# Chunks of 64 tokens instead of 128 in a delta-rule kernel: attention products as 64x64 tiles, and an inverse grown from diag(beta)

## Chip, cores and metric

The kernel runs on one core of a Trainium2 chip. The metric is the device time of one execution in microseconds (us). PE is TensorE, DVE is VectorE, ACT is ScalarE, POOL is GpSimd.

## The reference

Four batch elements with eight heads, 768 tokens and head size 48 go through the delta rule in float32. The result, 3072 tokens of width 384, goes through a block gated by a cosine with a hidden width of 2048.

```python
k_n = k / (np.linalg.norm(k, axis=-1, keepdims=True) + 1e-06)
for t in range(S):                       # state: (B, H, D, D)
    y[:, :, t] = q_t @ state
    v_old = k_t @ state
    state = state + beta_t * outer(k_t, v_t - v_old)
x = y.transpose(0, 2, 1, 3).reshape(B * S, H * D)
h = x @ w_in
out = (h * cos(h)) @ w_out               # float32
```

## The kernel before

In a chunk of C = 128 tokens, u = (I + A)^-1 (beta v - beta K S), y = Q S + mask(Q K^T) u and S += K^T u, where A is the part of beta K K^T below the diagonal. The inverse X is built from diagonal blocks that double in size. A *unit* is one chunk of one batch element with its 8 heads; there are 24. Two heads of size 48, padded to 64, share the 128 partitions. The even and odd heads ("parities") form two chains:

```python
def gram(par, lhs, rhs, name):                 # 64 rows, 128 columns
    rows = slice(DP * par, DP * par + DP)
    p = bank("att", [128, NP, 128], name)
    for j in range(NP):                        # NP = 4 heads of this parity
        nc.tensor.matmul(p[:, j], lhs[rows, j], rhs[rows, j])
    return p
# ... a = gram(kb_t, k_t), xt and x: identity minus pairs, by masks on DVE and POOL
for i, m in enumerate(LEVELS):                 # 2, 4, 8, 16, 32, 64
    for j in range(NP):
        nc.tensor.matmul(p_w[:, j], a[:, j], xt[:, j])
    nc.vector.tensor_tensor(out=wt, in0=p_w, in1=mask4(4 + i), op=ALU.mult)
    yield
    for j in range(NP):
        nc.tensor.matmul(p_xt[:, j], x[:, j], wt[:, j])
    # ... p_x = wt^T x, except at the last level
    nc.vector.tensor_tensor(out=xt, in0=xt, in1=p_xt, op=ALU.subtract)
    nc.vector.tensor_tensor(out=x, in0=x, in1=p_x, op=ALU.subtract)
    yield
```

Three streams are merged by their `yield`s: this preparation of unit n+1, the recurrence over chunks of unit n, and the gated block of two finished units (`p_h = w_in^T x`, the cosine on ACT and DVE, `p_o = g^T w_out`). The compiler's scheduler then orders each engine's instructions again: ready work of a later step may fill a gap.

## Time and profile before

| | before |
|---|---|
| time, median of 3 runs | 1667.6 us (1667.6 to 1669.3) |
| period of a unit in the steady part | 64.9 us |
| units 0 to 3 (the opening) | 287.6 us |
| PE busy in the span | 95% |

The period is the distance between the first query transposes of units 4 and 23 in the timeline, over 19. These are windows of the trace of the kernel before, one in the opening and one in the steady part; the columns are the window, its length, each engine's busy time with its number of instructions, the granted clock, DMA's share and its rate:

```profile
core 0: us, PE busy (x) PEld busy (x) DVE busy (x) ACT busy (x) POOL busy (x), PEclk, DMA share, GB/s
...
100.00:200.00 100.00, 84.92 (x564) 80.16 (x565) 91.95 (x184) 5.63 (x11) 31.86 (x27) 0.80 0.21 60
...
400.00:600.00 200.00, 199.31 (x1436) 176.84 (x1435) 104.13 (x167) 36.65 (x63) 35.45 (x30) 1.00 0.06 13
```

In the opening DVE is the busiest engine, 92 of 100 us, since it also narrows the weights.

### The profile page before, as it was taken

How to read it: one execution, taken by the hardware profiler on the slowest of the kernel's cores; microseconds unless marked ns; L12 is line 12 of the kernel's file. 1: busy time of each engine (PE TensorE's matmuls, PEld its weight loads, DVE VectorE, ACT ScalarE, POOL GpSimd, SP SyncE). 2: the span in 40 equal slices, each digit the busy share in tenths (PEclk: the TensorE clock that was granted, in tenths of full speed). 3: DMA queues.
4: the chain of work that ended last, by engine and by line, in shares of the span. 5: the costliest groups of instructions: out<-in, count | busy, mean ns of one | idle time of the engine just before them, and what ended most of it. 6: DMA issues, size and time to landing. Idle time of an engine off the chain costs nothing.

```text
span 1665.8 us, 25603 instructions
## 1 busy us (share of the span) xinstructions
PE 1588.9 (95%) x11214; PEld 1418.7 (85%) x11214; DVE 936.8 (56%) x1559; ACT 309.9 (19%) x530; POOL 326.8 (20%) x291
## 2 busy tenths in 40 slices
PE   4778989999999999999999999999999999999998
PEld 3778889889889889889889889989988988988965
DVE  4999866456456446446546545545545645644612
ACT  1010022122112112112203202202202202211222
POOL 7242250220220211202202202102122022011000
PEclk9978879999999999999999999999999999999999
DMA  7222000000000000000000000000000000000000
GB/s 161 85 72 76 25 15 6 15 15 6 20 15 6 20 15 6 20 15 6 10 19 12 10 10 20 10 10 20 10 11 20 1 10 6 1 6 6 1 10 10
DMA packets 82673, 33.87 MB, mean 20 GB/s; under 512 B 75744, under 2 KB 78816, under 8 KB 82560
## 3 DMA queue, kind: packets, MB, share of 16 engines
q1 hardware_dynamic: 82560, 32.22, 8.0%
q8 instruction: 88, 1.44, 0.4%
q14 instruction: 25, 0.20, 0.0%
HBM read 27.49 MB, written 4.72 MB: 19 GB/s over the span
## 4 chain that ended last, share of the span: by engine, by line
PE 78%; DVE 10%; POOL 6%; ACT 2%; issue 2%; DMA 0%; POOLq 0%; SPq 0%
PE p_o L422 15%; PE p_xt L288 14%; PE p_w L282 13%; PE p_h L393 13%; PE p_x L292 11%; PE p_y L363 2%; POOL xt L270 2%; POOL x L273 2%; PE p_u L329 1%; PE p_a L260 1%; POOL x L272 1%; PE p_t L247 1%; PE p_y L354 1%; PE p_qk L260 1%; DVE wt L284 1%
## 5 line engine op out<-in xcount | busy, mean ns | idle before, releaser
L288 PE MATMUL p_xt<-wt,x 128*128 128x128 f32 x2304 | 313.6, 281 | 24.1 <-DVE wt L284 23.7
L282 PE MATMUL p_w<-xt,a 128*128 128x128 f32 x2304 | 302.9, 281 | 24.6 <-POOL xt L270 19.9
L282 PEld LDWEIGHTS p_w<-xt,a 128*128 128x128 f32 x2304 | 285.5, 196 | 45.2 <-POOL xt L270 23.2
L288 PEld LDWEIGHTS p_xt<-wt,x 128*128 128x128 f32 x2304 | 289.4, 194 | 38.6 <-DVE wt L284 32.6
L284 DVE TENSOR_TENSOR wt<-p_w,masks 128x512 f32<-128x512 f32 x288 | 194.1, 688 | 208.1 <-PE p_w L282 207.9
L393 PE MATMUL p_h<-x_ffn,w_in 128*128 128x256 f32 x1152 | 280.5, 386 | 6.6 <-DVE g L414 6.1
L422 PE MATMUL p_o<-w_out,g 128*128 128x384 f32 x768 | 264.9, 488 | 0.9 <-DVE g L414 0.9
L292 PE MATMUL p_x<-x,wt 128*128 128x128 f32 x1920 | 255.5, 276 | 0.0
L393 PEld LDWEIGHTS p_h<-x_ffn,w_in 128*128 128x128 f32 x1152 | 211.1, 194 | 33.9 <-issue 4.6
L292 PEld LDWEIGHTS p_x<-x,wt 128*128 128x128 f32 x1920 | 235.7, 193 | 0.0
L293 DVE TENSOR_TENSOR xt<-xt,p_xt 128x512 f32<-128x512 f32 x240 | 164.4, 685 | 76.4 <-PE p_xt L288 75.8
L422 PEld LDWEIGHTS p_o<-w_out,g 128*128 128x128 f32 x768 | 138.5, 190 | 78.8 <-PE p_h L393 1.3
L404 DVE SCALAR_TENSOR_TENSOR r<-turns,p_h 128x512 f32<-128x512 int32 x96 | 66.0, 687 | 218.6 <-ACT turns L402 218.6
L297 DVE TENSOR_TENSOR x<-x,p_x 128x512 f32<-128x512 f32 x240 | 163.9, 683 | 24.4 <-PE p_x L292 21.9
L237 POOL TENSOR_TENSOR kb<-kp,bt 128x384 f32<-128x384 f32 x24 | 24.6, 1028 | 646.1 <-PE p_t L247 646.0
L402 ACT ACTIVATE turns<-p_h 128x512 int32<-128x512 f32 x96 | 57.3, 597 | 376.3 <-PE p_h L393 343.5
L230 POOL TENSOR_TENSOR knrm<-ksum,half 128x8 f32<-128x8 f32 x24 | 39.8, 1661 | 277.8 <-DVE ksum L226 277.8
L414 DVE TENSOR_TENSOR g<-r,p_h 128x512 f32<-128x512 f32 x96 | 65.7, 684 | 44.3 <-ACT r L411 42.8
L272 POOL TENSOR_TENSOR x<-a,masks 128x512 f32<-128x512 f32 x48 | 61.5, 1281 | 146.0 <-ACT a L266 143.6
L410 ACT ACTIVATE r<-r 128x512 f32<-128x512 f32 x96 | 60.5, 631 | 109.2 <-DVE r L407 109.2
L407 DVE SCALAR_TENSOR_TENSOR r<-turns,r 128x512 f32<-128x512 int32 x96 | 69.6, 725 | 0.5
L411 ACT ACTIVATE r<-r,halfpi 128x512 f32<-128x512 f32 x96 | 69.3, 722 | 2.8
(76 smaller groups left out, 1335.8 us busy)
## 6 DMA issues: line engine op xcount, KB each, us to landing
pairs<-in_moe_w_in_dram SPq DMA_DIRECT2D x12, 512.0 KB, 4.0
pairs<-in_moe_w_out_dram SPq DMA_DIRECT2D x16, 384.0 KB, 3.1
kp<-in_k_dram SPq DMA_DIRECT2D x24, 192.0 KB, 2.8
qp<-in_q_dram SPq DMA_DIRECT2D x24, 192.0 KB, 2.8
vp<-in_v_dram SPq DMA_DIRECT2D x24, 192.0 KB, 2.6
out_dram<-o SPq DMA_DIRECT2D x24, 192.0 KB, 1.9
masks<-mask_consts SPq DMA_DIRECT2D x1, 640.0 KB, 3.9
beta_rows<-in_beta_dram SPq DMA_DIRECT2D x1, 96.0 KB, 4.2
```

Source lines behind the costliest of these rows:

```text
L272: nc.gpsimd.tensor_tensor(out=x, in0=a, in1=mask4(2), op=ALU.mult)
L282: nc.tensor.matmul(p_w[:, j], a[:, j], xt[:, j])
L284: nc.vector.tensor_tensor(out=wt, in0=p_w, in1=mask4(4 + i), op=ALU.mult)
L288: nc.tensor.matmul(p_xt[:, j], x[:, j], wt[:, j])
L292: nc.tensor.matmul(p_x[:, j], wt[:, j], x[:, j])
L293: nc.vector.tensor_tensor(out=x_t[:, par] if last else xt, in0=xt, in1=p_xt, op=ALU.subtract)
L297: nc.vector.tensor_tensor(out=x, in0=x, in1=p_x, op=ALU.subtract)
L393: nc.tensor.matmul(p_h[:, i], w_in[:, t, (f + i) * 128 : (f + i + 1) * 128], x[:, t], start=(t == 0), stop=(t == KT - 1),)
L404: nc.vector.scalar_tensor_tensor(out=r, in0=turns, scalar=-PI2_HI, in1=p_h, op0=ALU.mult, op1=ALU.add)
L407: nc.vector.scalar_tensor_tensor(out=r, in0=turns, scalar=-PI2_LO, in1=r, op0=ALU.mult, op1=ALU.add)
L411: nc.scalar.activation(r, r, AF.Sin, bias=halfpi, scale=-1.0)
L422: nc.tensor.matmul(p_o, gs[f // 4][:, f % 4, i * C : (i + 1) * C], w_out[:, f], start=(f == 0), stop=(f == FT - 1),)
```

## The change

A chunk is 64 tokens, and two batch elements fill the 128 partitions, one in each half. Every attention product is then a 64x64 tile, placed by the row half of its operands and the partition half of its output. The inverse starts at X = diag(beta) on the plain Gram matrix, so beta k, its transposes and the POOL masks go. The core of the diff:

```diff
-C = 128
-LEVELS = (2, 4, 8, 16, 32, 64)
+C = 64
+LEVELS = (1, 2, 4, 8, 16, 32)
...
+    TILES = ((0, 0), (1, 1), (0, 1), (1, 0))      # (row half, output half)
...
+        for j in range(NP):
+            for par, i in TILES:
+                nc.tensor.matmul(p_g[half(i), par, j],
+                    kq_t[rows48(par), 0, j, half(i)], kq_t[rows48(par), :, j, half(i)])
...
+        def product(p, lhs, rhs):
+            for h in range(H):
+                for i in range(2):
+                    nc.tensor.matmul(
+                        p[half(i), h], flat(lhs)[half(i), h], flat(rhs)[half(i), h])
+        xt = x = dg                                # diag(beta)
+        for n_level, m in enumerate(LEVELS):
+            p_w = bank("one", [128, H, C], "p_w")
+            product(p_w, g, xt)
+            nc.vector.tensor_tensor(out=flat(wt), in0=p_w, in1=mask8(2 + n_level), op=ALU.mult)
+            yield
+            product(p_x[:, 0], x, wt)
+            if not last:
+                product(p_x[:, 1], wt, x)
+            # ... xt_new = xt - p_x[:, 0]; x_new = x - p_x[:, 1]
```

The recurrence is rewritten in the same way: `p_kq` for K S and Q S and `p_s` for the state's update use all four TILES, `p_u` and the rest of y the two diagonal ones. The gated block is unchanged.

## The prediction

> **What bounds the kernel now.** I first read the page's busy shares and the slices, then its chain that ended last, then the groups by line, and last the timeline of a steady stretch. The busy shares and the chain:
>
> ```profile
> span 1665.8 us, 25603 instructions
> PE 1588.9 (95%) x11214; PEld 1418.7 (85%) x11214; DVE 936.8 (56%) x1559; ACT 309.9 (19%) x530; POOL 326.8 (20%) x291
> PE 78%; DVE 10%; POOL 6%; ACT 2%; issue 2%; DMA 0%; POOLq 0%; SPq 0%
> ```
>
> PE is busy 95% of the span with 11,214 matmuls and as many weight loads, and 78% of the last chain is PE. DVE is at 56%, DMA nowhere. So the kernel is bound by PE, and the question is only what one matmul instruction costs. The groups by line:
>
> ```profile
> L288 PE MATMUL p_xt<-wt,x 128*128 128x128 f32 x2304 | 313.6, 281 | 24.1 <-DVE wt L284 23.7
> L282 PE MATMUL p_w<-xt,a 128*128 128x128 f32 x2304 | 302.9, 281 | 24.6 <-POOL xt L270 19.9
> L393 PE MATMUL p_h<-x_ffn,w_in 128*128 128x256 f32 x1152 | 280.5, 386 | 6.6 <-DVE g L414 6.1
> L422 PE MATMUL p_o<-w_out,g 128*128 128x384 f32 x768 | 264.9, 488 | 0.9 <-DVE g L414 0.9
> L292 PE MATMUL p_x<-x,wt 128*128 128x128 f32 x1920 | 255.5, 276 | 0.0
> ```
>
> The program has 24 units x 2 parities x 6 levels x 4 heads = 1152 products p_w, the profile 2304: an fp32 product is two PE instructions, each with its own weight load. I call such a load with its matmul a pair. The means (281, 386, 488 ns) are latencies that overlap; the cost is the distance between starts, which the timeline gives:
>
> ```profile
> 704.08 1.03 PE L337 MATMUL p_s<-u,kp 128*128 128x96 f32 x8
> 704.95 1.08 PE L288 MATMUL p_xt<-wt,x 128*128 128x128 f32 x8
> 705.87 1.06 PE L292 MATMUL p_x<-x,wt 128*128 128x128 f32 x8
> 706.76 1.06 PE L288 MATMUL p_xt<-wt,x 128*128 128x128 f32 x8
> 707.65 1.06 PE L292 MATMUL p_x<-x,wt 128*128 128x128 f32 x8
> 709.44 2.75 PE L422 MATMUL p_o<-w_out,g 128*128 128x384 f32 x8
> ```
>
> Eight p_xt start at 706.76 and the next group at 707.65: 0.89/8 = 0.111 us a pair. p_s, with only 96 moving columns, takes the same (0.87/8), so up to 128 columns a pair costs the load of its 128 stationary columns. p_o: (2.75-0.488)/7 = 0.323 us for 384 columns. p_h: the same timeline has 12 in 2.76 us, (2.76-0.386)/11 = 0.216. A unit of 128 tokens and 8 heads thus has 48 Gram pairs, 272 of the inverse and 56 of the recurrence, 376 x 0.111 = 41.7 us; 15 transposes (one instruction each) x 0.109 = 1.6; the gated block 48 x 0.216 + 32 x 0.323 = 20.7. The sum is 64.0 us; units in the steady part follow each other every 64.8 us (first transpose of a unit at 288 us, nineteen units later at 1520). So PE time explains the period with 0.8 us left over. 21 such periods are 1361 us; the other 305 us are the opening, where DVE narrows the weights (in the table of windows DVE is busy 92 of the 100 us from 100 us on), and the tail.
>
> **What the Trainium skill says.** "TensorE: Matmul & The Clock Gate", section LDWEIGHTS: a weight load takes its column count over 1.2 ns, whatever the rows; 128 columns give 106.7, and the 109 to 111 ns above agree. So 64 columns should give some 53. The same page, Part 3, The mechanism: matmuls in different row groups run at the same time, starting some 4 ns apart. The kernel before shows it where its two parities (row halves) meet in the Gram products:
>
> ```profile
> 684.33 0.72 PE L260 MATMUL p_at<-kb_t,k_t 64*128 64x128 f32 x5
> 685.00 0.27 PE L260 MATMUL p_a<-k_t,kb_t 64*128 64x128 f32 x1
> 685.00 0.27 PE L260 MATMUL p_at<-kb_t,k_t 64*128 64x128 f32 x1
> 685.11 0.27 PE L260 MATMUL p_a<-k_t,kb_t 64*128 64x128 f32 x1
> 685.11 0.27 PE L260 MATMUL p_at<-kb_t,k_t 64*128 64x128 f32 x1
> ```
>
> Alone, five p_at in a row are 0.11 us apart; here a p_a of the other half starts with each, so two pairs go in 0.11 us. "TensorEngine Tiling (Array Packing)", Key Properties: changing the tiling mode drains the engine. The trace agrees: from the last p_o at 686.76 + 1.56 - 0.49 = 687.83 to the first 64-row p_qk at 688.25 it takes 0.42 us instead of 0.32, and the next p_qk another 0.1 late; leaving again costs as much, some 0.35 us for a round trip (estimate). Lastly the first page's section "Wait — 56ns, not 53.3ns?" gives a floor of about 25 ns from start to start of matmuls, and about 62 ns each if the sequencer decodes in software. No stretch of this trace keeps a rate above two pairs in 0.11 us, so it doesn't show the floor.
>
> **The change part by part.** A unit is still 1024 token-heads (64 tokens, 16 heads of two batch elements), so there are still 24 units, and the gated block keeps its 80 pairs and 20.7 us.
>
> - Inverse: 16 products of 64x64 for 8 of 128x128. Pairs: (16x6 + 16x6 + 16x5) x 2 = 544 instead of 272. The two batch elements sit in the two row halves and alternate, so two run at once. At half the columns a pair takes 0.056 us in its half, and 0.028 with two halves. I take 0.033, for imperfect pairing: 544 x 0.033 = 18.0 us instead of 30.2.
> - Gram: one set of 16 products (32 pairs) with 128 moving columns, instead of 24 (48 pairs): 32 x 0.111/2 = 1.8 us instead of 5.3.
> - Recurrence: 64 + 32 + 32 + 32 = 160 pairs instead of 56: 5.3 us instead of 6.2.
> - Transposes: 11 instead of 15, 1.2 us.
> - Mode changes: small products now stand between pieces of the gated block at some 9 places a unit instead of 2: 9 x 0.35 = 3.2 us, instead of 0.7.
> - PE in sum: 18.0 + 1.8 + 5.3 + 1.2 + 20.7 + 3.2 = 50.2 us.
> - DVE (off the path): 17 steps of the inverse instead of 34 at 0.69 us, so 11.7 instead of 23.5; the gated block's r, r, g 4 x 2.1 = 8.4; the rest some 3: 23 us of a 50 us unit.
> - POOL loses three mask operations of 1.3 us of each parity and is far off the path. DMA moves the same bytes in packets of the same 192 bytes; each transfer is split in two.
> - New waits: there is one chain a unit instead of two that take turns. A level is p_w 1.1, mask 0.7 + 0.4 of latency, half of p_x 1.1, subtraction 0.7 + 0.4: 4.4 us; six levels 26, with the norms, transposes and Gram ahead some 35 us. That is shorter than 50, and the schedule fills gaps with the gated block (the p_o group of 8 is split into 4 and 4 around the Gram products at 683 to 688 us). The single buffer shared by p_w, p_u and p_z, and DVE's queue, leave some gaps open: I put 3 us a unit, chosen, not measured.
>
> A period is then 53 us. Outside the 21 periods, the opening three units lose 3 x 17 x 0.69 = 35 us of DVE work and some PE work: 305 - 45 = 260. The time is 21 x 53 + 260 = **1373 us**.
>
> **Rivals.**
>
> 1. The two halves do not overlap in a sustained way. A pair is 0.056 us, attention 736 x 0.056 = 41 us as before, and a unit 1.2 + 20.7 + 41 + 4 = 67: 1670 to 1720 us, nothing won. For it: only short stretches of overlap are seen. Against it: there it is complete.
> 2. The issue of instructions becomes the bound: 827 matmuls a unit instead of 471, with loads. At 0.045 us a pair the period is some 61 us, the time some 1550. For it: no rate like it is in the trace, and the floors cited.
> 3. The single chain's waits become the bound: PE has 29 us of attention and 21 of filler, but fillers come at the wrong moments. If half of 12 waits of 1.1 us stay open, a unit is 57 us and the time 1455.
> 4. Everything works at 0.028 with few gaps: 48 us a unit, 1265 us.
>
> **Range and chances.** The four give 1265 to 1720; I hold the overlap likely (it was seen) at a rate between 0.028 and 0.045. Hence 1370, 8 in 10 from 1265 to 1560. Faster by over 2% (below 1634) fails only in rival 1 or with rivals 2 and 3 together: 0.88; within 2% 0.05; slower 0.07.
>
> **What would show each step.** Starts of p_w and p_x in the timeline, two at once, 32 in 1.0 to 1.1 us, confirm the rate; 1.8 us for 32 shows rival 1, an even 40 to 50 ns between single starts rival 2. The period between first transposes should be 50 to 57 us. PE idle before p_x on DVE wt should be 1 to 4 us a unit; much more is rival 3. DVE's busy time should fall from 937 to some 640 us, the inverse's DVE steps from 816 to 408 in number. PE instructions should be some 19,900. The prediction is wrong if a 64-column load costs more than half a 128-column one, or if mode changes cost much more than 0.35 us.

## More of the kernel before

In the steady part PE is never free: 199.3 of 200 us.

## The result, and the profile after

The changed kernel takes 1239.2 us (median of 4 runs, 1237.4 to 1245.5). Its ratio to the kernel before is 0.743, 95% interval 0.742 to 0.745. A ratio here is the mean time of one kernel's fast runs over that of the other's of the same rounds, so it is not quite the ratio of the medians. The change is faster by a quarter, and the time lies below the lower end of the predicted range (1265).

| | before | predicted | after |
|---|---|---|---|
| period of a unit, us | 64.9 | 53 | 46.9 |
| the rest, span less 21 periods, us | 303 | 260 | 250 |
| opening (units 0 to 3), us | 287.6 | | 229.4 |
| DVE busy, us | 937 | 640 | 611 |

So nearly the whole miss is in the period: 21 x 6.1 = 128 us. From the page after, the busy shares, the chain that ended last and the largest groups:

```profile
span 1235.5 us, 41854 instructions
...
PE 1136.5 (92%) x19669; PEld 888.0 (72%) x19669; DVE 611.4 (49%) x1113; ACT 283.6 (23%) x482; POOL 132.8 (11%) x137
...
PE 80%; ACT 2%; DVE 1%; issue 0%
...
L433 PE MATMUL p_h<-x_ffn,w_in 128*128 128x256 f32 x1152 | 299.1, 395 | 3.4 <-DVE g_ffn L454 2.9
...
L462 PE MATMUL p_o<-w_out,g_ffn 128*128 128x384 f32 x768 | 281.9, 500 | 0.6 <-ACT o L472 0.6
...
L309 PE MATMUL p_w<-xt,g 64*64 64x64 f32 x3840 | 143.9, 222 | 41.5 <-DVE xt L328 41.5
...
L309 PE MATMUL p_x<-wt,x 64*64 64x64 f32 x3840 | 142.3, 225 | 15.1 <-DVE wt L319 13.9
```

PE still carries the chain. 3840 instructions p_w (and 768 more on the first level) take less busy time than 2304 did, because they overlap: the mean of one, 222 ns, is only a latency. The cost is in the timeline of one unit, PE alone:

```profile
601.83 1.15 PE L358 MATMUL p_kq<-st,kq_t 48*64 48x48 f32 x64
602.91 0.66 PE L276 MATMUL p_t<-ident,kp 128*128 128x128 f32 x4
...
606.52 1.10 PE L284 MATMUL p_g<-kq_t 48*64 48x128 f32 x32
607.55 1.56 PE L462 MATMUL p_o<-w_out,g_ffn 128*128 128x384 f32 x4
...
623.69 1.56 PE L462 MATMUL p_o<-w_out,g_ffn 128*128 128x384 f32 x4
625.18 1.15 PE L309 MATMUL p_x<-wt,x 64*64 64x64 f32 x32
626.16 1.10 PE L309 MATMUL p_x<-x,wt 64*64 64x64 f32 x32
627.10 1.09 PE L403 MATMUL p_kq<-u,tt 64*64 64x48 f32 x32
628.05 1.15 PE L309 MATMUL p_w<-xt,g 64*64 64x64 f32 x32
629.13 2.85 PE L462 MATMUL p_o<-w_out,g_ffn 128*128 128x384 f32 x8
```

From 626.16 to 627.10 there are 32 pairs: 0.94/32 = 0.029 us each, half of the 0.056 that a half-wide pair should take alone. The group p_kq of 64 takes 1.08 us, 0.017 a pair, so four tiles run at once there. No group of these lines has an idle time in brackets: after p_w the scheduler has put 4 to 8 instructions p_o, long enough for DVE's step. Here is the steady window of the changed kernel, columns as above:

```profile
400.00:600.00 200.00, 199.31 (x3499) 155.48 (x3499) 92.54 (x160) 51.63 (x88) 14.60 (x16) 1.00 0.09 18
```

PE idles for 0.7 us in 200, as before the change.

### The profile page after: what moved, and what is told of

Same layout as the page of the kernel before. It is cut to its first block, busy times and chain, and to the rows that moved or that the text cites. A ratio compares the mean times of both kernels' runs of the same rounds, so it can differ in the third digit from the quotient of the medians.

```text
span 1235.5 us, 41854 instructions
## 1 busy us (share of the span) xinstructions
PE 1136.5 (92%) x19669; PEld 888.0 (72%) x19669; DVE 611.4 (49%) x1113; ACT 283.6 (23%) x482; POOL 132.8 (11%) x137
## 4 chain that ended last, share of the span: by engine, by line
PE 80%; ACT 2%; DVE 1%; issue 0%
PE p_o L462 22%; PE p_h L433 20%; PE p_x L309 18%; PE p_w L309 11%; PE p_u L379 2%; PE p_kq L403 2%; PE p_g L284 2%; PE p_t L276 1%; PE p_kq L358 1%; PE p_s L391 1%; DVE r L444 1%; DVE r L447 1%; PE p_z L421 1%; ACT turns L442 1%; ACT r L450 1%; ACT kq_t L277 0%
## 5 line engine op out<-in xcount | busy, mean ns | idle before, releaser
L462 PE MATMUL p_o<-w_out,g_ffn 128*128 128x384 f32 x768 | 281.9, 500 | 0.6 <-ACT o L472 0.6
L462 PEld LDWEIGHTS p_o<-w_out,g_ffn 128*128 128x128 f32 x768 | 135.6, 189 | 74.4 <-issue 1.7
L309 PEld LDWEIGHTS p_w<-xt,g 64*64 64x64 f32 x3840 | 126.0, 135 | 81.4 <-DVE xt L328 44.3
L309 PE MATMUL p_w<-xt,g 64*64 64x64 f32 x3840 | 143.9, 222 | 41.5 <-DVE xt L328 41.5
L309 PEld LDWEIGHTS p_x<-wt,x 64*64 64x64 f32 x3840 | 125.6, 138 | 56.9 <-issue 31.1
L309 PE MATMUL p_x<-wt,x 64*64 64x64 f32 x3840 | 142.3, 225 | 15.1 <-DVE wt L319 13.9
L319 DVE TENSOR_TENSOR wt<-p_w,masks 128x512 f32<-128x512 f32 x144 | 98.6, 685 | 71.5 <-PE p_w L309 70.4
L309 PE MATMUL p_x<-x,wt 64*64 64x64 f32 x3072 | 108.8, 222 | 0.0
L309 PEld LDWEIGHTS p_x<-x,wt 64*64 64x64 f32 x3072 | 100.8, 139 | 0.0
L333 DVE TENSOR_TENSOR x<-x,p_x 128x512 f32<-128x512 f32 x96 | 65.3, 680 | 0.0
```

The source lines that it names most:

```text
L309: nc.tensor.matmul(p[half(i), h], flat(lhs)[half(i), h], flat(rhs)[half(i), h])
L319: nc.vector.tensor_tensor(out=flat(wt), in0=p_w, in1=mask8(2 + n_level), op=ALU.mult)
L333: nc.vector.tensor_tensor(out=flat(x_new), in0=flat(x), in1=p_x[:, 1], op=ALU.subtract)
L462: nc.tensor.matmul(p_o, gs[f // 4][:, f % 4, i * 128 : (i + 1) * 128], w_out[:, f], start=(f == 0), stop=(f == FT - 1),)
```

## The experiments

The theory that I tested: the period fell because tiles in different parts of the array run at the same time, two in the inverse and four in the Gram and state products; the chain's waits, though 1 us each, are filled with the gated block. The rivals: the halved width alone is the gain; four tiles are no faster than two; the waits are small; DVE's lighter load is the gain. Each kernel gave a correct result. All medians are of 4 or 5 runs.

| kernel | us | ratio to before | period | opening |
|---|---|---|---|---|
| changed | 1239.2 | 0.743 | 46.9 | 229 |
| halves_apart | 1547.7 | 0.928 | 58.6 | 303 |
| two_tiles | 1261.0 | 0.756 | 48.0 | 230 |
| gated_last | 1480.3 | 0.887 | 34.9 (attention alone) | 231 |
| visit_small | 1324.5 | 0.795 | 50.6 | 232 |
| visit_large | 1292.9 | 0.774 | 49.1 | 235 |
| dve_doubled | 1279.6 | 0.767 | 47.7 | 257 |
| pairs_start | 1216.6 | 0.729 | 45.3 | 241 |
| crossed | 1153.8 | 0.692 | 42.9 | 229 |
| crossed_again | 1157.6 | 0.693 | 42.9 | 229 |
| crossed_pairs | 1182.2 | 0.709 | 43.9 | 228 |
| before_paired | 1707.9 | 1.024 | 67.0 | 287 |

### halves_apart: the overlap of the row halves taken away by order alone

```diff
-            for h in range(H):
-                for i in range(2):
+            for i in range(2):
+                for h in range(H):
                     nc.tensor.matmul(p[half(i), h], ...)
```

> The changed kernel, but each group of the inverse's products is issued for one row half first and then for the other. Theory A (the two row halves run at the same time and that is the main gain): a pair costs 0.056 us instead of the 0.029 seen, 544 of them a unit, +14.5 us less some overlap where the halves meet: a period of 58 to 61 us instead of 46.4, 1500 to 1575 us in all. Rival B (the gain is the halved width of each load and matmul, and PE's queue pairs up what it finds): no change, 1240 us.

Measured: 1547.7 us, a period of 58.6, so +11.7 us a unit. That is within what theory A said. The timeline of this run, PE alone:

```profile
604.18 1.69 PE L309 MATMUL p_x<-wt,dg 64*64 64x64 f32 x29
605.65 0.27 PE L309 MATMUL p_x<-dg,wt 64*64 64x64 f32 x1
605.70 0.22 PE L309 MATMUL p_x<-wt,dg 64*64 64x64 f32 x1
605.76 0.22 PE L309 MATMUL p_x<-dg,wt 64*64 64x64 f32 x1
605.76 0.22 PE L309 MATMUL p_x<-wt,dg 64*64 64x64 f32 x1
605.82 0.22 PE L309 MATMUL p_x<-dg,wt 64*64 64x64 f32 x1
605.82 0.22 PE L309 MATMUL p_x<-wt,dg 64*64 64x64 f32 x1
605.87 1.67 PE L309 MATMUL p_x<-dg,wt 64*64 64x64 f32 x29
```

The latency of one is 0.22 us, so 29 take (1.69 - 0.22)/28 = 0.053 us each. But these 29 are all 16 instructions of one half and 13 of the other, and where the first half ends some overlap. A window that shows matmuls of the second half alone (605.35 to 605.60) gives the rate of one half:

```profile
605.18 0.63 PE L309 MATMUL p_x<-wt,dg 64*64 64x64 f32 x8
```

That is (0.63 - 0.22)/7 = 0.058 us a pair: half of before's 0.111, and twice the changed kernel's 0.029. Only where one half ends and the other begins do two start together, and there a matmul starts ahead of three that stand before it in the program. Rival B is refuted: the queue doesn't find distant partners, and the instructions must alternate in the program. Without the overlap in the inverse the change would have won 7%, not 26%.

### two_tiles: four tiles or two

```diff
-        for j in range(NP):
-            for par, i in TILES:
+        for pair in (TILES[:2], TILES[2:]):
+          for j in range(NP):
+            for par, i in pair:
```

This was done in the Gram products, in p_kq and in p_s.

> The changed kernel, but the Gram products, the products with the state and the state's update are issued so that only the two diagonal or the two crossed tiles meet, not four. Theory A (four tiles run at once; the prediction had counted two): the Gram group goes from 1.0 to 1.9 us and the group of 64 with the state from 1.1 to 1.9, +1.9 us a unit, 1285 us. Rival B (four tiles are no faster than two; the surplus over the prediction comes from elsewhere): 1240 us.

Measured: 1261.0 us, +1.1 us a unit. The direction is that of theory A, at half of its size. In this run's timeline:

```profile
610.32 1.88 PE L360 MATMUL p_kq<-st,kq_t 48*64 48x48 f32 x64
...
615.74 1.59 PE L285 MATMUL p_g<-kq_t 48*64 48x128 f32 x32
```

p_kq went from 1.15 to 1.88 us as expected, but p_g only from 1.10 to 1.59 and not to 1.9. Four tiles beat two, and this explains some 1.1 us of the miss, not the 1.9 that I gave it.

### gated_last: the filler taken away

```diff
-            streams.append((gen, N_FFN // 2 + n % 2))     # the gated block, merged
...
+    tc.strict_bb_all_engine_barrier()
+    for p in range(NU // 2):
+        for _ in ffn(p):
+            pass
```

> The changed kernel, but the gated block runs after all attention, behind a barrier; same instructions. Theory A (one chain a unit has about 1.1 us of DVE latency after each group, which the gated block's matmuls fill): PE idles in the attention part, a period there is 33 to 36 us with 22 us of PE work, 1350 to 1420 us in all. Rival B (the chain's waits are small by themselves, or successive units fill them): 25 us a period, fewer changes of tile size, 1150 to 1190 us.

Measured: 1480.3 us. The period of attention alone is 34.9 us, as theory A said (33 to 36), and rival B's 25 is refuted; the total is above A's 1350 to 1420 mostly because I had set nothing aside for the opening, whose four units take 231 us and not 4 x 34.9 = 140. A window of this run in the attention part, columns as above:

```profile
400.00:600.00 200.00, 144.30 (x4307) 131.28 (x4304) 79.98 (x143) 21.80 (x41) 20.57 (x23) 0.97 0.11 21
```

And PE's waits from 300 to 900 us (the waiter, what it waited for, us in total, times, longest):

```profile
PE p_x L309 <- DVE wt L319: 52.1, 68, 0.8
PE p_w L309 <- DVE xt L328: 47.6, 68, 0.9
```

PE idles 28% of the attention part, 0.28 x 34.9 = 9.7 us a unit. The two waits shown are of 0.7 to 0.8 us on average and make up 99.7 us in 600, or 5.8 us a unit; the rest are like waits of other groups of PE for DVE and ACT. So the waits are real, though shorter than the 1.1 us that theory A gave, and the merged kernel hides them: the same program with the gated block in between idles 0.35%.

### visit_small and visit_large: what a change of tile size costs

```diff
+                if f % 2 == 0:            # 8 times in each p_o, 192 in all
+                    nc.tensor.matmul(p_ow[0:64, DM:DM+64], ident[0:64, 0:64],
+                        ident[0:64, 0:64], start=False, stop=True, skip_group_check=True)
```

The control uses `p_ow[:, DM:DM+64], ident, ident[:, 0:64]`, over the whole array.

> The changed kernel with one unused 64x64 product (two pairs) put between every second pair of the output products p_o, 192 in all, in columns of the bank that nobody reads. Theory A (a visit to the other tile size costs some 0.34 us: 0.09 and an exposed load each way): 192 x (0.34 + 0.06) = 77 us more, less where the product falls beside a group of small ones anyway; 60 to 80 us. Rival B (only the drain of 0.1 us counts): 192 x 0.2 = 38 us. To be set against the run with the large product.

> The same with an unused product over the full 128 rows and columns, 64 moving columns, so that the tile size does not change: two pairs of 0.111 us by theory A, 192 x 0.22 = 43 us more. It is the control: what the small one costs beyond it, plus the difference of the pairs themselves, is the change of tile size.

Measured: +85.3 and +53.7 us. Both are some 10 us over theory A, and the difference, 31.6 us, is close to the 34 that it gave. In the built program's order of PE's instructions the changed kernel changes tile size 595 times, the small product brings 384 changes and the large one 36, that is 192 and 18 round trips. With 0.12 us for the two small pairs (2 x 0.058) and 0.22 for the large ones, 31.6 = 192 x (0.12 - 0.22) + 174 t, and t is some 0.3 us a round trip. The two traces show a visit directly, the small one first:

```profile
1246.68 1.56 PE L463 MATMUL p_o<-w_out,g_ffn 128*128 128x384 f32 x4
1248.17 0.33 PE L472 MATMUL p_o<-ident 64*64 64x64 f32 x2
1248.43 1.56 PE L463 MATMUL p_o<-w_out,g_ffn 128*128 128x384 f32 x4
...
1221.54 1.51 PE L463 MATMUL p_o<-w_out,g_ffn 128*128 128x384 f32 x4
1222.89 0.33 PE L472 MATMUL p_o<-ident 128*128 128x64 f32 x2
1223.06 0.86 PE L463 MATMUL p_o<-w_out,g_ffn 128*128 128x384 f32 x2
```

Four p_o alone take 4 x 0.323 = 1.29 us. With the small product they take 1.75, with the large one 1.52, so 0.46 and 0.23 more. The large one costs just its two pairs; the small one, less 0.12 for its pairs, costs 0.34 us for the round trip, against the 0.35 that the prediction had read from two gaps of the trace before. The changed kernel makes 595/2/24 = 12.4 round trips a unit, not the 9 that I had counted: some 4 us.

### dve_doubled: DVE's load put back

```diff
+            again = work.tile([128, 2, NP, C], FP, name="again")
+            nc.vector.tensor_tensor(
+                out=flat(again), in0=p_w, in1=mask8(2 + n_level), op=ALU.mult)
```

The same was done for the two subtractions.

> The changed kernel with each of the inverse's 17 DVE steps done a second time into a tile that nobody reads, so DVE has the inverse's work of the kernel before (34 steps of 0.69 us a unit). Theory A (DVE is off the path; its halving is no part of the gain): within 2% of 1239, 1240 to 1265 us, DVE busy 611 + 280 us. Rival B (half the gain came from DVE's latency in the chain): 1350 us or more.

Measured: 1279.6 us, +40 us, so neither theory fits. The split tells why: the opening went from 229 to 257 us (+28), the period only from 46.9 to 47.7 (+0.8, 15 us over 19 units). DVE is off the path in the steady part, as theory A has it, but it is on it in the opening, where it also narrows weights. Some 28 of the 58 us that the change gains in the opening thus come from fewer DVE steps there, where the prediction had 35; what the other 30 come from was not tested.

### pairs_start: the second part of the change undone

```diff
-LEVELS = (1, 2, 4, 8, 16, 32)
+LEVELS = (2, 4, 8, 16, 32)
...
-        xt = x = dg
+        # kb = beta k and its transposes again; A and A^T as Gram products
+        nc.vector.tensor_tensor(out=xt[:, par], in0=p_g[:, par, :, 1], in1=..., op=ALU.mult)
+        nc.gpsimd.tensor_tensor(out=xtf, in0=xtf, in1=mask8(0), op=ALU.add)
+        nc.gpsimd.tensor_tensor(out=xf, in0=g, in1=mask8(n_masks - 1), op=ALU.mult)
+        nc.gpsimd.tensor_tensor(out=xf, in0=xf, in1=mask8(0), op=ALU.add)
```

> The changed kernel with the second part of the change undone: beta k and its transposes again, A and its transpose as Gram products, the start from pairs by masks on POOL, and five levels of doubling instead of six. PE loses 96 pairs and two visits and gets 32 pairs, 4 transposes and a visit. Theory A (PE's time decides, and growing from diag(beta) costs PE more than it saves): -2.8 -0.7 +0.6 +0.4 +0.3 = -2.2 us a unit, 1185 to 1200 us. Rival B (the longer way through POOL ahead of the chain shows, so the plain Gram matrix is a gain): 1250 us or more.

Measured: 1216.6 us, ratio 0.729, 23 us faster than the changed kernel. The period fell by 1.6 us (31 us over 19 units; A said 2.2), while the opening grew by 12 us, which A had left out. So growing the inverse from diag(beta) is a small loss here, and the gain of the change lies in its other part, the chunks of 64 with their tiles. What in the longer start costs the 12 us was not tested.

### crossed: four tiles in the inverse as well

In the changed kernel the inverse uses only the two diagonal tiles. Here x and wt of a batch element lie in the other half than its g and xt. p_w then writes crosswise, p_x[:, 0] crosswise back, and p_x[:, 1] stays in its half. Issued in turn, the two p_x groups use all four tiles, and no two row halves write the same bank and partitions.

```diff
-        xt = x = dg
+        xt, x = dg, dgs                    # dgs: diag(beta) of the other batch element
-            product(p_w, g, xt)
+            product([(p_w, g, xt, True)])                 # True: into the other half
-            product(p_x[:, 0], x, wt)
-            if not last:
-                product(p_x[:, 1], wt, x)
+            jobs = [(p_x[:, 0], x, wt, True)]
+            if not last:
+                jobs.append((p_x[:, 1], wt, x, False))
+            product(jobs)
```

> The changed kernel, but x and wt are kept in the row half that g and xt of the same batch element do not use. p_w then takes the two crossed tiles, and the two groups of p_x, issued in turn, take all four. Theory A (four tiles at once, as in the Gram group): the 64 pairs of p_x go in 1.1 us instead of 1.9 in five levels, -4.0 us a unit, 1140 to 1160 us. Rival B (the queue or the issue of instructions limits at two pairs in 0.058 us): 1240 us.

> The crossed kernel once more, on the chip of the run beside it, to compare the two: 1150 to 1160 us.

Measured: 1153.8 and 1157.6 us, ratio 0.69; the period fell by 4.0 us, just as theory A said. Its timeline, where each line holds two matmuls that start within 0.01 us of each other:

```profile
500.32 0.22 PE L323 MATMUL p_x<-wt,x 64*64 64x64 f32 x2
500.33 0.23 PE L323 MATMUL p_x<-x,wt 64*64 64x64 f32 x2
500.38 0.23 PE L323 MATMUL p_x<-wt,x 64*64 64x64 f32 x2
500.39 0.23 PE L323 MATMUL p_x<-x,wt 64*64 64x64 f32 x2
...
500.86 0.23 PE L323 MATMUL p_x<-x,wt 64*64 64x64 f32 x2
```

From 500.33 to 500.86 there are nine steps of 0.059 us with four matmuls in each: 0.015 us a pair. One tile alone takes a pair each 0.058 us (halves_apart), so the four of a step lie in four tiles. No floor of the instructions' issue shows at that rate. This is the fastest kernel.

### crossed_pairs: both gains together

```diff
+                for swap in range(2):      # A's Gram product, once for each half
+                    nc.tensor.matmul(
+                        p_a[half(1 - i if swap else i), par, swap, j], ...)
```

> Both gains together: x and wt in crossed halves, and the start from pairs with five levels; A's Gram product is made twice, once for each half. Against the crossed kernel PE loses level one (0.9 + 1.1 us) and two visits (0.7) and gets two Gram groups (0.5 each), 4 transposes (0.4) and a visit (0.35): -0.9 us a unit in the steady part, and some 12 us more in the opening, as with the start from pairs alone. Theory A: 1140 to 1155 us. Rival B (the longer start shows, since crossed already has idle gaps of 2% on PE): 1155 to 1175 us, no gain.

Measured: 1182.2 us, 24.6 us slower than the crossed kernel beside it, and above what both theories said. PE has less to do, but its steady window shows:

```profile
400.00:600.00 200.00, 189.19 (x3597) 139.55 (x3596) 87.96 (x156) 55.12 (x97) 37.72 (x33) 0.97 0.11 21
```

PE idles 10.8 us of 200 (the crossed kernel 3.8), at a clock of 0.97 instead of 1.00. In the waits of the same window PE's largest is p_x for DVE's wt, up to 2.8 us at once. The saved PE time came back as waits and a lower clock; that the schedule no longer had filler at the right moments is my reading, which no run tested. Two gains that each hold alone did not add.

### before_paired: the overlap alone, in the kernel before

```diff
-            for j in range(NP):
-                nc.tensor.matmul(p[:, j], lhs[rows, j], rhs[rows, j])
+            for j in range(NP):
+                for i in range(2):         # both parities in turn, each to its own bank
+                    rows = slice(DP * i, DP * i + DP)
+                    nc.tensor.matmul(both[i][:, j], lhs[rows, j], rhs[rows, j])
```

> The kernel before, unchanged but for the order of the Gram products: the two parities, which lie in different row halves, are issued in turn instead of one after the other. Theory A (the overlap of row halves works in the old kernel too, and is a matter of order alone): 48 pairs a unit at half of 0.111 us instead of nearly all of it, -2.0 to -2.6 us a unit, 1605 to 1620 us. Rival B (128-column products don't overlap for long): 1667 us.

Measured: 1707.9 us, 2.4% slower than the kernel before, which neither theory foresaw. From its timeline:

```profile
695.62 1.16 PE L264 MATMUL p_a<-k_t,kb_t 64*128 64x128 f32 x16
696.61 1.06 PE L264 MATMUL p_at<-kb_t,k_t 64*128 64x128 f32 x16
...
700.18 1.99 PE L334 MATMUL p_u<-rhs,x_t 128*128 128x48 f32 x16
...
703.17 2.49 POOL L275 TENSOR_TENSOR xt<-xt,masks 128x512 f32<-128x512 f32 x2
...
704.49 2.07 PE L287 MATMUL p_w<-xt,a 128*128 128x128 f32 x8 [2.32 <-POOL xt L275]
...
706.36 4.56 PE L427 MATMUL p_o<-w_out,g 128*128 128x384 f32 x8
```

Two windows of the same stretch; the third figure from the right is the granted clock:

```profile
702.00:706.00 4.00, 1.68 (x9) 1.55 (x9) 0.00 (x0) 0.48 (x1) 3.66 (x3) 0.65 0.00 0
706.00:712.00 6.00, 6.00 (x23) 4.01 (x23) 0.85 (x2) 0.00 (x0) 0.00 (x0) 0.67 0.00 0
```

The overlap itself works: 16 p_a take (1.16 - 0.27)/15 = 0.059 us each instead of 0.111, some 2.5 us a unit. But now both parities reach POOL together, and its six mask steps delay xt, so PE waits 2.3 us. From 400 to 1400 us such waits take 35.3 us, against 4.8 in the kernel before. And the granted clock falls: cut finer, the trace has 0.99 from 702.0 to 703.2 us, 0.50 from there to 710.0 and 1.00 after it (the mean from 400 to 600 us is 0.96, and 1.00 in the kernel before). The next 8 p_o take 4.56 us instead of 2.75. The wait and the clock's loss, 2.3 + 1.8 + some 1.0 on p_w, outweigh the gain in this stretch; the period grew by 2.1 us. "TensorE: Matmul & The Clock Gate", Part 1 of the Trainium skill, describes such a drop: the clock is halved after an idle window of about 3.4 us. Here it is halved 1.0 us after PE's wait began, and the whole wait is 2.3 us.

## Why the prediction was right or wrong

The bound, the direction and the mechanism were right: PE stays the bound, the two halves overlap, and gaps are filled with the gated block. The sum's terms, in us a unit:

| term | predicted | measured | from |
|---|---|---|---|
| inverse, 544 pairs | 18.0 | 16.0 | 0.0294 us a pair in the timeline |
| Gram | 1.8 | 0.9 | p_g 606.52 to 607.55, less a tile change |
| recurrence | 5.3 | 3.5 | p_kq 1.08, p_u 0.97, y 0.95, p_s some 0.6, less a tile change |
| transposes and gated block | 21.9 | 21.9 | as before |
| changes of tile size | 3.2 | some 4.2 | 12.4 round trips of 0.34 |
| waits of the single chain | 3.0 | some 0.4 | what is left of 46.9 |
| sum | 53.2 | 46.9 | |

The steps that failed are sizes: three terms of the sum, each put too high. The first is the last of the list's points: "I put 3 us a unit, chosen, not measured". Where nothing fills the chain's waits they come to 9.7 us a unit (gated_last; rival 3's 12 waits of 1.1 us would be 13), but the scheduler hid nearly all of them, as it did in the kernel before, whose own 0.8 us left over should have warned me. That is 2.6 of the 6.3 us. The second, some 2.7 more, is the Gram and the recurrence: "32 x 0.111/2" and 0.033 for all 160 pairs counted two tiles, though the program's TILES name four; two_tiles shows 1.1 us of this directly; the rest, the rates that I chose too high, was not taken apart. The third is the inverse: "0.033, for imperfect pairing" against 0.029 is 2.0 us. Pairing was complete: 0.029 is half of the 0.058 of one half alone. The tile changes were under-counted, 9 for 12.4, by 1 us the other way.

The lower end of the range came from rival 4 ("everything works at 0.028 with few gaps: 48 us a unit"), which kept the two tiles for Gram and recurrence. With only two tiles at once there, two_tiles took 1261.0 us, close to that end. So even the best case was above what happened, and the range had no room below it. Rival 1 is refuted for the changed kernel's order. In another order (halves_apart) its rate does appear in the inverse, 0.058 us a pair, but the period is 58.6 us and not its 67, since the Gram and recurrence products still overlap. Rival 2 is refuted: crossed ran at 0.015 us a pair. Rival 3 is refuted for this kernel; waits of its kind come back in crossed_pairs and before_paired.

Of what was to show it: 32 p_x in 0.94 to 0.98 us (1.0 to 1.1 foretold), a period of 46.9 (50 to 57), PE's steady idle of under 0.2 us a unit (1 to 4), 408 DVE steps (408), 19,669 PE instructions (19,900), DVE busy 611 us (640).

## What to carry to other kernels

When products need only half the array's rows or columns, put independent ones into different row and column halves and let them alternate in program order: two tiles halve the cost of each pair and four quarter it, while the same products one half after the other only gain from their smaller width. A chain's waits cost nothing while a bound engine has other ready work, so estimate them from the idle time that the present schedule leaves, not from their length; but when the work of the bound engine shrinks, or when two chains start to ask for one slow engine at once, they come back, and with them a lower clock. Give a range's favourable end room below the best case that you have thought of.

## What the Trainium skill lacked or had wrong

- "TensorE: Matmul & The Clock Gate", section "Wait — 56ns, not 53.3ns?": its start-to-start floor of about 25 ns is stated without saying that it is one tile's, though the 4 ns between tiles that the prediction cites suggest so. Here four tiles sustained 0.015 us a matmul, each with its own load (crossed), so neither that floor nor the 62 ns of software decode bound these runs.
- The same page, Part 3, "The mechanism", calls matmuls strictly first in, first out in start and end. In halves_apart a group's first matmul of the other row half (605.65) started ahead of three of the group before it (605.70 to 605.82), which stand earlier in the built program. In the stretch shown this happens only where the products pass from one row half to the other, and by three.
- "TensorEngine Tiling (Array Packing)", Key Properties, says that a change of tiling mode drains the engine but gives no cost. Here a round trip between 128x128 and 64x64 cost some 0.3 us by the totals of visit_small and visit_large, and 0.34 by their timelines.
- The same page says nothing of program order. Tiles overlap only if they alternate closely: 0.029 us a pair in turn, 0.058 inside a stretch of 16 instructions of one half (halves_apart).
- "TensorE: Matmul & The Clock Gate", Part 1, gives an idle window of about 3.4 us before the clock is halved: here the granted clock was 0.50 for 6.8 us, from 1.0 us into a PE wait of only 2.3 us (before_paired).
